# One flag in a planned kernel: the casts of dense operands offered to ScalarE during attention as well

## The chip, the cores and the metric

The kernel runs on one core of a Trainium2 chip. The metric is the device time of one execution in microseconds (us). The engines are TensorE (PE; its weight loads are PEld), VectorE (DVE), ScalarE (ACT), GpSimd (POOL) and SyncE (SP), which issues all transfers between the chip's memory and the core.

## The reference

Two computations stand side by side in the output, 2048 rows by 2 x 1024 columns, all in 32-bit floats.

```python
# left half: attention, 32 heads of 32 columns, no mask
qkv = (x @ wqkv)                       # x 2048x1024, wqkv 1024x3072
scores = einsum("bhqd,bhkd->bhqk", q, k) * Dh ** -0.5
o = einsum("bhqk,bhkd->bhqd", softmax(scores), v)
a = o_as_2048x1024 @ wo
# right half: a Fourier mixing with the matrices given as inputs
p = x2 @ hid_re.T ; q = x2 @ hid_im.T
b = seq_re @ p - seq_im @ q            # 2048x2048 by 2048x1024, twice
out = concatenate([a, b], axis=-1)
```

## The kernel before

**The dense products** (the projections to q, k and v; the two stages of the Fourier mixing, called dense1 and dense2; the output projection, called project) are done in blocks by a scheme with seven products in place of eight, so many operands are first sums or differences of blocks. They run on TensorE in a fast 32-bit format (`F32R`). To keep the accuracy each operand is split in two: the high part is the operand rounded to that format, the low part is what is left. Three matmuls are then made, high by high, low by high, high by low. An operand tile is 128 x 512. Its way is: a load by SP into `raw` (line 437); where it is a sum, a second load `g` (line 446) and an addition on GpSimd or VectorE (line 453); then in `halves` the **cast to the high part** on VectorE (line 475) or on ScalarE (line 473), and the subtraction for the low part on GpSimd or VectorE (line 478). Stationary operands are called `h` and `l` and live in three buffers (`piece`), moving operands are called `slot` (`moving`). The results of the q and k projection pass through `halves` too; their high part is `vh` early in the kernel and `e` later. Line 389 is the matmul of every dense product, into the PSUM tiles `pd` and `psT`; lines 627 to 745 and 892 to 910 take the results out.

**Attention** goes head by head. Line 1193 makes a 128 x 1024 piece of scores in PSUM (`psS`, two buffers). VectorE takes the row maximum, negated, `negm` (line 1199). ScalarE makes exp and its row sums from it, in place (line 1202), which frees the buffer. From these come the softmax's maxima and sums. Line 1316 makes the scores once more, transposed, 128 x 512 (`psT`, two buffers), with the maxima folded in as extra rows. ScalarE makes exp of them into one of 27 tiles `pt` and `ptl` (line 1320). Line 1335 multiplies these by V into `pd`, three times for each head after 5, 5 and 6 of its 16 rows of tiles; lines 1346 and 1348 gather the sums in `ot`, line 1364 divides by the softmax's sums, line 1366 stores them to `o_d`. The projection's operands are loaded from `o_d`, and no load of them starts before the stores of all heads are issued and done.

**The order** is made by a planner when the program is built, and nothing is decided on the chip. Each operation is an `Op` with an engine, a cost in us, a rank and the operations that it waits for. `Plan` keeps a list for each engine of what is ready; an engine that is free takes the ready operation of lowest rank. The row maximum has rank 0 on VectorE and the exps have -1 and 0 on ScalarE. An operation may have a second engine (`other`), and then stands in both lists, with its own cost and rank in each: the engine that is free first takes it, and where both are free ScalarE is asked before VectorE. The additions and subtractions have GpSimd and VectorE in this way. A cast has VectorE (cost 0.415, rank 10 + number of its group) and, where `spare[0]` is true at the time when the operation is set up, ScalarE too (cost `ACAST` = 0.6, rank 25 + number of its group). Operations with `two=True`, casts among them, are kept by the planner from running on VectorE while GpSimd runs. TensorE's own order is made by the loop from line 1396: the attention's three streams S (psS), T (psT) and V (times V), and the list `fills` of all dense matmuls in order. A fill goes where no stream is ready, or where the dense part is behind the pace (`nf / (FILL - RES) <= done / ATT`). The projection is the end of that list.

`qkv` sets up its dense products in twelve steps. The first five make the blocks that the first heads need; the rest of `qkv`, then dense1 and dense2, are worked off while attention runs, from about 245 to 2790 us. Line 804 sets the flag at the head of each of the steps 0 to 9: true in steps 0 to 4, and false from step 5, after which it stays false until `behind` (line 1064) sets it true for the projection.

Of the kernel before, what the change touches and what calls it, by code (L numbers as in the profile page):

```python
# [210 lines left out]
def kernel(  # L211
# [253 lines left out]
    spare = [True]  # L465
# [18 lines left out]
    def piece(terms, store=None):  # L484

        box = {}
        raw, made, users = fetch([P, 4, P], terms, store)
        (o0, u0), (o1, u1) = HR.take(), LR.take()

        def tile_of(key):  # L490
            def get():
                if key not in box:
                    box[key] = parts.tile([P, 4, P], F32R, name=key, tag=key, bufs=3)
                return box[key]
            return get

        h, l = tile_of("h"), tile_of("l")
        made = halves(raw, made, users, h, l, (o0, o1), (u0, u1), (HR, LR))
        both = Both(u0, u1)
        return Piece(h, l, made, both)  # L500
# [66 lines left out]
    def qkv():  # L567
# [5 lines left out]
        def w_terms(p, q, s_d, s):  # L573
            return {
                1: lambda: [(1, q(0, 0), [])], 2: lambda: [(1, q(0, 1), [])], 4: lambda: [(1, q(1, 1), [])],
                5: lambda: [(1, q(1, 0), []), (1, q(1, 1), [])],
                6: lambda: [(1, q(1, 0), []), (1, q(1, 1), []), (-1, q(0, 0), [])],
                7: lambda: [(1, q(0, 0), []), (-1, q(1, 0), [])],
                3: lambda: [(1, q(0, 1), []), (-1, s_d, s)],
            }[p]()  # L580
# [18 lines left out]
        def load_x(x, k):  # L599
            where[0] = ahead if x < 5 else within  # L600
            p = STEPS[x][0]
            if x < 5:
                i = 8 * ((x + 1) % 2) + k
                i = i if i < 12 else 20 + i
            else:
                i = (8 * (x - 5) + k) % 12 if x < 11 else (16, 8)[k // 4] + k
            XS[x, k] = moving(i, x_terms(p, k, x >= 5), (tx_d[k], tx[k]) if x == 3 else (t1x_d[k], t1x[k]) if x == 2 else None)

        def load_v_weight(x, c):
            where[0] = ahead if x < 5 else within  # L610
            p = STEPS[x][0]
            WV[x, c] = moving((28 if x in (1, 3) else 12 if x == 10 else 0 if x == 11 else 36) + c, w_terms(p, lambda i, j: wv[i, 4 * j + c], sv_d[c], sv[c]), (sv_d[c], sv[c]) if p == 6 else None)

        def acc(i):
            box = {}

            def get():
                if "t" not in box:
                    box["t"] = vp.tile([P, 2, NB], F32, name=f"acc{i}")
                return box["t"]  # L620

            return [Acc(get, [], [], k) for k in range(2)]
# [161 lines left out]
        def qk_group(x, W, b, n):  # L784
            p = STEPS[x][0]
            early = x < 5
            h = FIRST.get(p)
            if p == 1 and n == 0:
                if early:
                    X[2 * b], X[2 * b + 1] = acc(b)  # L790
                else:
                    X[2 * b], X[2 * b + 1] = accs(15 + b - PAIRS)
            group(((chunk(W, c), (XS[x, 4 * n + c], whole)) for c in range(4)), 4,
                  gather(p, 2 * b + n, qk_result(b + 8 * h[0], 2 * h[1] + n, early) if h else None, early, None if b % 2 else SCALE))

        def v_group(x, t):
            p = STEPS[x][0]
            h = FIRST.get(p)
            s0 = t % 4 * P
            group((((XS[x, 4 * (t // 4) + c], lambda u, s0=s0: u[:, s0 : s0 + P]), (WV[x, c], whole)) for c in range(4)), 4,  # L800
                  gather(p, 16 + t, v_result(h[0], 8 * h[1] + t, x < 5) if h else None, x < 5))

        for x, (p, blocks, v) in enumerate(STEPS[:10]):
            spare[0] = x < 5
            for i, b in enumerate(blocks):
                where[0] = ahead if x < 5 else within
                W = piece(w_terms(p, lambda i, j: wqk[b + 8 * i][:, 4 * j : 4 * j + 4, :], sq_d[b], sq[b]), (sq_d[b], sq[b]) if p == 6 else None)
                if x == i == 0:
                    first = W
                    for k in range(4):  # L810
                        load_x(0, k)
                    qk_group(x, W, 0, 0)
                    continue
                if x == 0 and i == 1 or x > 5 and i == 0:
                    for k in range(4, 8):
                        load_x(x, k)
                qk_group(x, W, b, 0)
                if x == 0 and i == 1:
                    qk_group(x, first, 0, 1)
                qk_group(x, W, b, 1)  # L820
                if x == 0:
                    if i == 1:
                        for c in range(4):
                            load_v_weight(0, c)
                elif x < 5:
                    for k in range(8 * i // len(blocks), 8 * (i + 1) // len(blocks)):
                        load_x(x + 1, k)
                elif i < 4:
                    load_x(x + 1, i)
            for t in range(8 if v else 0):  # L830
                if p == 1 and t % 2 == 0:
                    X[16 + t], X[17 + t] = acc(PAIRS + t // 2)
                v_group(x, t)
                if x == 0:
                    load_x(1, t)
                if t < 4 and x < 4:
                    load_v_weight(x + 1, t)
            where[0] = within
            if x == 4:
                for u in ahead[0].users + slots[28:]:  # L840
                    att_gate.extend(u)
                for i in range(12, 20):
                    slots[i] = list(att_gate)
            if x == 9:
                for c in range(4):
                    load_v_weight(10, c)
# [514 lines left out]
    def result(h, e, po, ouse):  # L1361
# [4 lines left out]
        o_st[h].append(op("SP", ISSUE, lambda: nc.sync.dma_start(o_d[h // 4][:, h % 4, :], po["o"]), [a], [ouse], -2, 256))  # L1366

    qkv()
    for w in (1, 0):
        for j in range(4):  # L1370
# [135 lines left out]
```

## Time and profile before

| | |
|---|---|
| three timed runs, median | 2978.28 us (2978.08 to 2978.9) |
| profiled execution, first to last instruction (span) | 2976.1 us |
| TensorE busy | 2950.9 us, 99% |
| VectorE busy | 2403.6 us, 81% |
| ScalarE busy | 2285.9 us, 77% |
| GpSimd busy | 868.7 us, 29% |
| casts on VectorE (line 475), whole span | 615 |
| casts on ScalarE (line 473), whole span | 161, none between 180 and 2800 us |

For the profiled execution the profile gives its span and no other time; the runs' median is 2.2 us above it.

How to read the lines that follow. A row of the groups names line, engine and operation, then the tile written and the tiles read, their shapes and the count; then busy time in us and the mean of one in ns; then the idle time of the engine just ahead of these instructions and what ended it. A row of busy times by stretch has the stretch, its length, then for PE, PEld, DVE, ACT and POOL the busy time with the number of instructions, then the granted TensorE clock, the share of the DMA engines and GB/s; where it is asked of one line only, the busy time is that of this line. A row of the waits names who waited, for whom, the us in total, how often, and the longest. A row of the view of one line has least, median and longest duration in ns, and the start of the first and last. A row in order of time has start, duration, engine, line, operation, and in brackets the idle time before it with what ended it. A row of the chain of waits has start, length, engine, tile, line and count.

### The profile page before, as it was taken

The page shows a single profiled execution, that of the slowest core. Times are in us where ns is not written, and L with a number is a line of the kernel's source. Part 1 is how long each engine was busy: PE and PEld are TensorE (multiplying, and loading weights), DVE is VectorE, ACT ScalarE, POOL GpSimd, SP SyncE. Part 2 cuts the span into 40 slices and gives each one's busy share as a digit, 9 for nine tenths or more (in the row PEclk, how much of TensorE's full clock was granted, in tenths as well). Part 3 has the DMA queues.
Part 4 walks back from the last instruction along what each step waited for, and adds up shares of the span by engine and source line. Part 5 has one row for each costly group of instructions (what it writes and reads, how often), then busy time and mean ns, then how long its engine had stood idle before and what let it go on. Part 6 is the DMA issues. An engine that isn't in the chain of part 4 may idle for free. (4 is left out here: it accounts for less than half of the span.)

```text
span 2976.1 us, 45423 instructions
## 1 busy us (share of the span) xinstructions
PE 2950.9 (99%) x14912; PEld 2136.2 (72%) x14912; DVE 2403.6 (81%) x3237; ACT 2285.9 (77%) x4314; POOL 868.7 (29%) x641
## 2 busy tenths in 40 slices
PE   9999999999999999999999999999999999999999
PEld 7886766777777777777777667677777666677787
DVE  7678889788877877777778898888777888887696
ACT  5347888888888888888888888888888888887431
POOL 2312425122212332131102443332012534342152
PEclk9999999999999999999999999999999999999999
DMA  9974658666625655554425775555334775555662
GB/s 347 357 228 161 196 181 284 220 218 227 209 74 193 193 155 160 172 177 149 153 87 170 226 226 166 162 165 164 113 110 137 228 248 174 160 181 179 229 229 98
DMA packets 376576, 558.56 MB, mean 188 GB/s; under 512 B 111100, under 2 KB 111100, under 8 KB 376220
## 3 DMA queue, kind: packets, MB, share of 16 engines
q1 hardware_dynamic: 376344, 555.68, 58.6%
q8 instruction: 120, 1.97, 0.3%
q14 instruction: 112, 0.92, 0.1%
HBM read 402.42 MB, written 153.11 MB: 187 GB/s over the span
## 5 line engine op out<-in xcount | busy, mean ns | idle before, releaser
L1199 DVE TENSOR_REDUCE negm<-psS 128x1 f32<-128x1024 f32 x1024 | 1240.6, 1219 | 194.8 <-PE psS L1193 189.6
L1202 ACT ACTIVATE psS<-psS,negm 128x1024 f32<-128x1024 f32 x1024 | 1170.7, 1143 | 104.2 <-DVE negm L1199 99.2
L1320 ACT ACTIVATE pt<-psT 128x512 f32<-128x512 f32 x1668 | 964.9, 654 | 270.7 <-PE psT L1316 268.6
L389 PE MATMUL pd<-slot,h 128*128 128x512 f32 x3368 | 1145.7, 390 | 1.2 <-DVE ot L1346 0.9
L1316 PE MATMUL psT<-qs,ks 128*128 128x512 f32 x2048 | 804.9, 396 | 0.0
L389 PEld LDWEIGHTS pd<-slot,h 128*128 128x128 f32 x3368 | 632.3, 188 | 133.7 <-DVE h L475 1.3
L389 PE MATMUL pd<-slot,l 128*128 128x512 f32 x1684 | 656.4, 390 | 0.7 <-POOL l L478 0.7
L1316 PEld LDWEIGHTS psT<-qs,ks 128*128 128x128 f32 x2048 | 381.6, 188 | 169.5 <-issue 62.9
L1193 PE MATMUL psS<-ks,qs 128*128 128x512 f32 x1552 | 476.2, 392 | 7.1 <-ACT psS L1202 6.5
L478 POOL TENSOR_TENSOR l<-raw,h 128x512 fp32r<-128x512 f32 x160 | 214.6, 1341 | 828.9 <-PE psT L1316 344.8
L1335 PE MATMUL pd<-pt,vt 128*32 128x512 f32 x3336 | 430.6, 594 | 0.2
L453 POOL TENSOR_TENSOR raw<-raw,g 128x512 f32<-128x512 f32 x216 | 285.7, 1329 | 439.1 <-issue 74.8
L389 PEld LDWEIGHTS pd<-slot,l 128*128 128x128 f32 x1684 | 316.2, 188 | 67.4 <-POOL l L478 1.0
L1193 PEld LDWEIGHTS psS<-ks,qs 128*128 128x128 f32 x1552 | 288.5, 188 | 76.4 <-ACT psS L1202 17.9
L478 POOL TENSOR_TENSOR slot<-raw,slot 128x512 fp32r<-128x512 f32 x143 | 206.6, 1453 | 432.9 <-DVE slot L475 203.1
L1335 PEld LDWEIGHTS pd<-pt,vt 128*32 128x32 f32 x3336 | 111.3, 110 | 230.2 <-issue 216.4
L1320 ACT ACTIVATE ptl<-psT 128x512 f32<-128x512 f32 x380 | 224.5, 654 | 59.9 <-PE psT L1316 59.5
L1202 ACT ACTIVATION_READ_ACCUMULATOR psS<-psS,negm 128x1 f32 x1024 | 266.6, 260 | 0.0
L389 PE MATMUL pd<-slot,slot 128*128 128x512 f32 x768 | 193.4, 390 | 0.0
L389 PEld LDWEIGHTS pd<-slot,slot 128*128 128x128 f32 x768 | 144.2, 188 | 30.8
L475 DVE CAST h<-raw 128x512 fp32r<-128x512 f32 x321 | 148.8, 464 | 14.8 <-PE pd L389 10.7
L1348 DVE TENSOR_TENSOR ot<-ot,pd 128x512 f32<-128x512 f32 x64 | 44.0, 687 | 144.0 <-PE pd L1335 143.9
(121 smaller groups left out, 2254.6 us busy)
## 6 DMA issues: line engine op xcount, KB each, us to landing
raw<-in_ct SPq DMA_DIRECT2D x224, 256.0 KB
g<-in_ct SPq DMA_DIRECT2D x128, 256.0 KB
qk_d<-e SPq DMA_DIRECT2D x52, 512.0 KB
qs<-qk_d SPq DMA_DIRECT2D x128, 192.0 KB
ks<-qk_d SPq DMA_DIRECT2D x128, 192.0 KB
raw<-ab_d SPq DMA_DIRECT2D x96, 256.0 KB
c<-u_d SPq DMA_DIRECT2D x88, 256.0 KB
g<-ab_d SPq DMA_DIRECT2D x80, 256.0 KB
```

What stands on the lines that cost most here:

```text
L389: nc.tensor.matmul(box["ps"], a[1]((a[0].hi, a[0].lo)[u]()), b[1]((b[0].hi, b[0].lo)[v]()), start=k == 0, stop=k == n - 1)
L453: (nc.gpsimd if e == "POOL" else nc.vector).tensor_tensor(out=dest(), in0=dest() if a is None else a.get(), in1=other["q"] if "q" in other ...
L475: nc.vector.tensor_copy(hi(), raw())
L478: (nc.gpsimd if e == "POOL" else nc.vector).tensor_tensor(out=lo(), in0=raw(), in1=f(hi()), op=ALU.subtract)
L1193: nc.tensor.matmul(p[:, i * NB : i * NB + NB], (QX[0] if own else QS[h % 2])[:, qt * P : qt * P + P], KS[h % 2][:, c * 1024 + i * NB : c * ...
L1199: nc.vector.tensor_reduce(out=ST["negm"][:, c, qt : qt + 1], in_=box["p"], axis=AX.X, op=ALU.max, negate=True)
L1202: nc.scalar.activation(box["p"], box["p"], AF.Exp, bias=ST["negm"][:, c, qt : qt + 1], accum_out=ST["sums"][:, c, qt : qt + 1])
L1316: nc.tensor.matmul(box["p"], KS[h % 2][:, t * P : t * P + P], QS[h % 2][:, j * NB : j * NB + NB], start=True, stop=True)
L1320: nc.scalar.activation(box["t"], box["p"], AF.Exp)
L1335: nc.tensor.matmul(po["p"][j * DH : j * DH + DH, :], VT[h][:, k, :], box["t"], start=(k == t0), stop=(k == t), tile_position=(0, j * DH),)
L1348: nc.vector.tensor_tensor(out=po["o"], in0=po["o"], in1=po["p"], op=ALU.add)
```

## The change

In `qkv`, line 804:

```diff
         for x, (p, blocks, v) in enumerate(STEPS[:10]):
-            spare[0] = x < 5
+            spare[0] = True
             for i, b in enumerate(blocks):
                 where[0] = ahead if x < 5 else within
```

The flag is then true from the start to the end. Every cast that is set up in the steps from 5 on, in dense1 and in dense2 is offered to ScalarE as well, with the cost and the rank that the first steps and the projection have. What is cast, added, subtracted, multiplied and stored is the same as before, on the same tiles; the planner makes a new order from it for all engines.

## The prediction

> **What bounds the kernel now.** I read the head of the page first, then busy times by stretch, then who waits for whom.
>
> ```profile
> span 2976.1 us, 45423 instructions
> ...
> PE 2950.9 (99%) x14912; PEld 2136.2 (72%) x14912; DVE 2403.6 (81%) x3237; ACT 2285.9 (77%) x4314; POOL 868.7 (29%) x641
> ```
>
> ```profile
> 74.00:148.00 74.00, 74.00 (x328) 61.29 (x327) 52.26 (x75) 26.05 (x44) 24.08 (x17) 1.00 0.98 359
> 245.00:2790.00 2545.00, 2530.19 (x13063) 1789.31 (x13065) 2066.16 (x2783) 2132.80 (x4059) 739.27 (x550) 1.00 0.57 178
> 2714.00:2791.00 77.00, 77.00 (x428) 51.93 (x426) 41.94 (x79) 40.44 (x76) 4.00 (x3) 1.00 0.53 165
> ```
>
> TensorE is idle for 2976.1 - 2950.9 = 25.2 us of the whole span, and its clock is full (the 1.00 in each stretch). A busy TensorE could still be one that creeps, so I check its pace: from 74 to 148 us 328 matmuls of 512 columns take 74 us, 0.226 us each, and the chain of waits on its last 130 us advances by 5.44 us for each 24 of them, 0.227 us:
>
> ```profile
> 2963.90 5.44 PE pd L389 x24
> ```
>
> So TensorE is the bound, and the change takes no matmul away. From 245 to 2790 us (attention) VectorE is idle for 2545 - 2066 = 479 us and ScalarE for 2545 - 2133 = 412 us. An engine relieved there gives time back only where TensorE waited for it:
>
> ```profile
> PEld psS L1193 <- ACT psS L1202: 30.7, 50, 1.7
> PEld psT L1316 <- ACT pt L1320: 9.7, 51, 0.3
> PEld psT L389 <- ACT slot L473: 6.3, 1, 6.3
> ```
>
> In the first row a score matmul into psS waits 50 times for an exp that has not yet read the bank; the second is the same for psT, 51 short waits. The third is the kernel's first matmul, before the change begins. 30.7 + 9.7 = 40.4 us, 1.4% of the span, is thus the ceiling of a gain, and all of it hangs on ScalarE. ScalarE in turn waits:
>
> ```profile
> ACT pt L1320 <- PE psT L1316: 268.6, 181, 6.7
> ...
> DVE ot L1348 <- PE pd L1335: 143.9, 58, 6.0
> ACT psS L1202 <- DVE negm L1199: 99.2, 136, 6.9
> DVE ot L1346 <- PE pd L1335: 67.0, 27, 4.3
> ```
>
> Two kinds of gap: 268.6 us in which it has no transposed score, and 99.2 us in which the row maximum (negm) from VectorE is late. The VectorE rows for ot show that a good part of the first kind is the P.V matmuls: 85 times (58 + 27) VectorE too stands still until they end, 211 us in all. While TensorE runs P.V it makes no scores, and both engines run dry together.
>
> **The change, part by part.** No instruction is added. A cast on offer to both engines goes to the one that the planner finds free first; it then writes down another order for all engines, the queues of DMAs included.
>
> ```profile
> 245.00:2790.00 2545.00, 276.52 (x576) 1.00 0.57 178
> ```
>
> That is line 475 in attention: 576 casts on VectorE, 0.480 us each. *How many move* the trace of before cannot show; the bounds are none and 576. ScalarE is idle for 412/2545 = 16% of the stretch, exps go before casts in its list, and VectorE, which also has the casts in its list, is idle beside it while P.V runs. I take 16% of 576 = 93, say 100.
>
> ```profile
> L475 DVE CAST h<-raw 128x512 fp32r<-128x512 f32 x321 | 148.8, 464 | 14.8 <-PE pd L389 10.7 <-issue 1.8 <-PE psT L389 1.0
> ...
> L453 DVE TENSOR_TENSOR raw<-raw,g 128x512 f32<-128x512 f32 x156 | 122.5, 791 | 18.8 <-DMA raw<-t_d 3.5 <-DMA raw<-in_xb 3.0 <-DMA g<-in_ct 2.9
> ...
> L475 DVE CAST slot<-raw 128x512 fp32r<-128x512 f32 x230 | 121.2, 541 | 1.5 <-DMA raw<-ab_d 0.6 <-PE pd L389 0.2
> ...
> L473 ACT ACTIVATE slot<-raw 128x512 fp32r<-128x512 f32 x54 | 32.2, 628 | 84.2 <-PE psT L389 33.2 <-DMA raw<-in_wo 17.0 <-issue 15.1
> ...
> L475 DVE CAST e<-e 128x512 fp32r<-128x512 f32 x52 | 26.5, 510 | 0.2
> ...
> L473 ACT ACT_TABLE_LOAD x1 | 1.3, 1283 | 0.7 <-PEq L1499 0.7
> ```
>
> *VectorE loses* 100 x 0.48 = 48 us of 2066. VectorE isn't the bound, so by itself this is worth 0.
>
> *ScalarE gains* 100 x 0.63 = 63 us beside 412 us of idle time. The cover is the gaps above and, for an exp that is pushed back, TensorE's dense matmuls, which the planner deals out meanwhile. There is no reload of function tables to pay: the whole span has one load, though copies (line 473) and exps alternate before 180 us. The planner charges 0.60 us for such a cast and the row says 0.63: 100 x 0.03 = 3 us of lateness that the written order does not know of. I charge all 3 us to TensorE.
>
> *A stall goes.* Casts on VectorE run 379/420/1514 ns (least, median, most) in one group:
>
> ```profile
> L475 DVE CAST h<-raw x307: 379/420/1514, 253.1 to 2784.1; 128x512 fp32r<-128x512 f32 x154
> L475 DVE CAST slot<-raw x217: 378/420/1552, 246.6 to 2756.8; 128x512 fp32r<-128x512 f32 x109
> ```
>
> ```profile
> 248.43 1.29 POOL L478 TENSOR_TENSOR e<-e 128x512 fp32r<-128x512 f32 x1
> ...
> 248.52 1.48 DVE L475 CAST slot<-raw 128x512 fp32r<-128x512 f32 x1
> ...
> 249.92 1.21 DVE L1199 TENSOR_REDUCE negm<-psS 128x1 f32<-128x1024 f32 x1
> ...
> 250.31 0.74 PE L1193 MATMUL psS<-ks,qx 128*128 128x512 f32 x2 [0.59 <-ACT psS L1202]
> ```
>
> The cast of 248.52 stands 1.06 us too long while a GpSimd subtraction runs, the next maximum starts late, and soon a score matmul waits. What casts lose in this way, against the 420 ns of the median: 321 x 0.044 + 230 x 0.121 + 52 x 0.090 = 14.1 + 27.8 + 4.7 = 47 us. With 100 of 576 moved, 8 us of it go. The additions of line 453 are stretched too, 791 ns against 0.69 us of one with no other by its side:
>
> ```profile
> 1298.18 0.69 DVE L453 TENSOR_TENSOR raw<-raw,g 128x512 f32<-128x512 f32 x1 [3.03 <-DMA raw<-in_xb]
> ```
>
> That is 156 x 0.10 = 16 us, and such delays and late loads together make the 30.7 us; at 30.7/(47 + 16) = 0.5 us of stall for each us of stretch, which is generous, 8 us give **-4 us**. Ends: 0, and -23 us if all casts moved (47 x 0.5). Late next is then the same maximum behind a stretched addition or subtraction, which stay where they are.
>
> The Trainium skill (page "SBUF — State Buffer", section "SBUF: two separate sides") says that VectorE and GpSimd share one pair of ports as an exclusive lock, the loser blocked for the whole instruction, while ScalarE has ports of its own. The pair at 248 us agrees, the cast ending just after the subtraction. By that rule each moved cast is one collision less; it is rival A below.
>
> *A wait is added.* ScalarE works in order: a cast whose raw tile is not there holds every exp behind it, those hold the psS and psT banks, and those hold TensorE. On VectorE the casts hardly wait for data (0.6 us for DMA raw<-ab_d in the row of slot<-raw): taken over, 0 us. Upper end: the additions on VectorE, which wait 18.8/156 = 0.12 us each, so 100 x 0.12 = 12 us. I take **+1 us**, near the cast rows since it is the same operation on the same tiles.
>
> *The rest is dealt again.* The order on all engines changes, SP's loads and stores with it, and the stalls that have nothing to do with casts fall elsewhere. The nearest rows give no sign to it: 0, with ends of half the 30.7 us to either side, 15 us.
>
> *The end.* The last head's P.V ends, then dense matmuls cover the way to the projection's operands:
>
> ```profile
> 2787.10 4.03 PE L1335 MATMUL pd<-pt,vt 128*32 128x512 f32 x34
> ...
> 2813.03 0.63 ACT L473 ACTIVATE slot<-raw 128x512 fp32r<-128x512 f32 x1 [1.34 <-DMA raw<-o_d]
> ...
> 2819.57 2.65 PE L389 MATMUL psT<-slot,slot 128*128 128x512 f32 x11
> ```
>
> From 2791.1 to 2819.6 lie 28.5 us of dense work; the operands' casts end at 2813.7, 6 us early. Before it, from 2714 to 2791, the last head has 77 us with ScalarE busy for 40.4, so 37 us of room. Attention may thus run some 37 + 6 = 43 us late before TensorE stands still at the end. 63 us of casts, most of them in gaps, stay below that: 0.
>
> **Sum** against the profiled execution: 2976.1 + 3 - 4 + 1 + 0 + 0 = 2976.1 us. The runs' median, 2978.28, is 2.2 us above this span, and that stays: 2978.3, rounded to **2978.5 us**. About 0.2%, 6 us, is what a measurement of this kernel can tell from no change.
>
> **Rivals.**
>
> A, *the collisions were the stall* (faster). ScalarE takes 250 casts or more: 250/576 x 47 = 20 us of stretch go, the cleared VectorE also makes the maxima earlier, and 8 to 20 of the 30.7 us vanish: 2958 to 2970, taken at 2966. For it: the pair at 248 us, and the maximum as what ScalarE waits for 136 times. Against it: VectorE is idle in the P.V gaps too and will often be first.
>
> B, *ScalarE's queue is held* (slower). Casts wait on loads and GpSimd sums as the additions do: 12 us, plus as much again from exps that find a cast begun just before them (100 x 0.12): 2978.3 + 12 to + 24, taken at 2992. It decides as soon as a cast's input lands later than ScalarE reaches it, in over a third of the moved casts. For it: TensorE's only sizeable waits are for ScalarE. Against it: ScalarE's own gaps of 1.5 us (268.6/181).
>
> C, *attention ends late* (slower). With 250 casts, half of them before an exp that was due, 125 x 0.63 = 79 us of delay meet 43 us of room: +36 us, 3014. It needs more than 43/0.63 = 68 casts that nothing hides.
>
> D, *the planner gives ScalarE next to nothing*, since VectorE is always first: 2978.3.
>
> **How the numbers follow.** Forecast (within 6 us) 0.44, D 0.05, A 0.21, B 0.20, C 0.10. So faster 0.21, same 0.49, slower 0.30. The forecast's own range is 2972 to 2985. For 8 in 10, A is taken in down to 2962 and B in full and C up to 3004; what is left out is the foot of A (0.05) and most of C (0.08).
>
> **What would show it.** Line 473 with some 100 more casts and line 475 with as many fewer; the exps' waits for psT and negm shorter by some 60 us together; the wait of psS matmuls for exps within 15 us of 30.7; TensorE's count of matmuls unchanged. A shows in that wait below 20 us and hardly any cast above 1 us; B in ScalarE waiting at line 473 for DMA or GpSimd inside attention, and that wait above 42 us; C in a gap of TensorE between the last P.V and the projection's first matmul. I am wrong if line 473 takes more than half of the casts, or if the order moves the loads so that TensorE waits for an operand (line 389).

## The result, and the profile after

The changed kernel takes **2984.63 us** (median of 17 runs, 2982.59 to 2987.87), the kernel before 2977.59 us in the same runs: a ratio of 1.0027, 95% interval 1.002 to 1.0034, some 7 to 8 us slower. The profiled execution went from 2976.1 to 2981.9 us, 5.8 more. First the page of the changed kernel and the view of line 473 inside attention:

```profile
span 2981.9 us, 45564 instructions
...
PE 2951.7 (99%) x14912; PEld 2141.9 (72%) x14912; DVE 2338.3 (78%) x3086; ACT 2349.1 (79%) x4444; POOL 894.9 (30%) x662
```

```profile
L473 ACT ACTIVATE h<-raw x54: 616/636/863, 246.1 to 2787.7; 128x512 fp32r<-128x512 f32 x54
L473 ACT ACTIVATE slot<-raw x47: 616/634/875, 246.6 to 2742.7; 128x512 fp32r<-128x512 f32 x47
...
L473 ACT ACTIVATE e<-e x7: 619/631/644, 249.5 to 737.8; 128x512 fp32r<-128x512 f32 x7
...
  PE pd L389: 9.5, 8
  DVE raw L453: 8.9, 11
```

54 + 47 + 7 = 108 casts went to ScalarE in attention. ScalarE stood still ahead of them, mainly for a free buffer (9.5 us) and for an addition on VectorE (8.9 us). TensorE makes the same matmuls at the same pace, so the question is where it waited. Its busy time in three stretches, before and then after:

```profile
200.00:800.00 600.00, 595.03 (x2995) 423.14 (x2994) 511.35 (x691) 495.69 (x939) 185.71 (x136) 1.00 0.66 214
800.00:2800.00 2000.00, 1990.16 (x10315) 1410.87 (x10314) 1601.12 (x2158) 1665.26 (x3171) 564.63 (x422) 1.00 0.54 165
2800.00:2850.00 50.00, 50.00 (x223) 41.39 (x222) 48.11 (x62) 18.21 (x30) 23.71 (x15) 1.00 1.03 367
```

```profile
200.00:800.00 600.00, 588.97 (x2958) 416.85 (x2957) 489.95 (x640) 502.56 (x950) 190.84 (x141) 1.00 0.66 211
800.00:2800.00 2000.00, 1996.38 (x10360) 1424.83 (x10362) 1567.38 (x2074) 1715.27 (x3277) 587.49 (x439) 1.00 0.54 166
2800.00:2850.00 50.00, 45.25 (x199) 34.81 (x188) 38.54 (x49) 20.41 (x35) 17.28 (x11) 0.94 0.90 319
```

Idle time of TensorE: 5.0 to 11.0 us in the first heads, 9.8 to 3.6 us in the long middle, 0 to 4.8 us where the projection begins, there with a granted clock of 0.94 besides. On this order the change is thus not one effect but three, and two of them nearly cancel.

A busy TensorE hides part of a wait, as its matmuls overlap in the trace (each counts as busy for 0.39 us and starts 0.23 us behind the one before). So I also add up, from the starts of the matmuls in the trace, what each start is later than the pace allows (0.2265 us after the one before; 0.318 us into and 0.522 us out of a run of P.V; distances within 20 ns of that are left out). I call this **lateness**. By it the stretches change by +8.4, -10.9 and +8.4 us, with 0.3 us in the first 200 us together +6.2. Span less lateness is 2933 to 2936 us in all fourteen kernels, so lateness is nearly the whole difference between them.

The middle shows as shorter waits of score matmuls (30.7 us before), the end as new rows:

```profile
PEld psS L1193 <- ACT psS L1202: 19.9, 34, 1.6
PEld psT L1316 <- ACT pt L1320: 12.8, 47, 1.4
PEld psT L389 <- ACT slot L473: 8.0, 2, 6.7
PEld psT L389 <- DVE slot L478: 5.1, 4, 4.0
```

This is the end in order of time, in the changed kernel:

```profile
2799.41 2.76 PE L1335 MATMUL pd<-pt,vt 128*32 128x512 f32 x24
...
2817.01 2.48 PE L389 MATMUL psT<-slot,slot 128*128 128x512 f32 x10
...
2840.42 0.73 PE L389 MATMUL psT<-slot,slot 128*128 128x512 f32 x2 [0.87 <-ACT slot L473]
...
2844.76 4.63 PE L389 MATMUL psT<-slot,slot 128*128 128x512 f32 x10 [3.60 <-DVE slot L478]
```

The last P.V ends at 2802.2 us, 11 us later than before, and the projection's first product begins only 15 us behind it (2817.01), where it was 28.5 us. Counted from the trace, 5983 dense matmuls now stand ahead of the last P.V's last matmul, 5923 before: 60 fewer are left to cover the loads. The first product gets by with a wait of 0.28 us; the second, due at 2839.4 us, finds its operands missing.

### The profile page after: what moved, and what is told of

The parts are those of the page before. It is cut to its first block, busy times and chain, and to the rows that moved or that the text cites. A ratio compares the mean times of both kernels' runs of the same rounds, so it can differ in the third digit from the quotient of the medians.

```text
span 2981.9 us, 45564 instructions
## 1 busy us (share of the span) xinstructions
PE 2951.7 (99%) x14912; PEld 2141.9 (72%) x14912; DVE 2338.3 (78%) x3086; ACT 2349.1 (79%) x4444; POOL 894.9 (30%) x662
## 4 chain that ended last, share of the span: by engine, by line
PE 93%; DVE 3%; DMA 2%; ACT 1%; issue 1%; POOL 0%; SPq 0%; DVEq 0%; POOLq 0%; ACTq 0%
PE pd L389 42%; PE psT L1316 15%; PE psS L1193 15%; PE pd L1335 15%; PE psT L389 6%; ACT psS L1202 1%; DVE negm L1199 1%; DMA raw<-in_ct 0%; DVE raw L453 0%; DMA raw<-tx_d 0%; DVE slot L475 0%; DMA raw<-in_wd 0%; ACT pt L1320 0%; DVE slot L478 0%; DMA qk_d<-e 0%
## 5 line engine op out<-in xcount | busy, mean ns | idle before, releaser
L1202 ACT ACTIVATE psS<-psS,negm 128x1024 f32<-128x1024 f32 x1024 | 1175.8, 1148 | 60.0 <-DVE negm L1199 56.8
L1320 ACT ACTIVATE pt<-psT 128x512 f32<-128x512 f32 x1668 | 966.8, 658 | 248.5 <-PE psT L1316 247.6
L478 POOL TENSOR_TENSOR l<-raw,h 128x512 fp32r<-128x512 f32 x170 | 226.7, 1333 | 870.8 <-PE psT L1316 300.2
L453 POOL TENSOR_TENSOR raw<-raw,g 128x512 f32<-128x512 f32 x208 | 278.2, 1343 | 375.8 <-DMA raw<-in_ct 73.1
L478 POOL TENSOR_TENSOR slot<-raw,slot 128x512 fp32r<-128x512 f32 x160 | 229.0, 1441 | 439.0 <-ACT slot L473 219.4
L1193 PE MATMUL psS<-ks,qx 128*128 128x512 f32 x496 | 150.4, 394 | 2.0 <-ACT psS L1202 1.9
```

What stands on the lines that cost most here:

```text
L453: (nc.gpsimd if e == "POOL" else nc.vector).tensor_tensor(out=dest(), in0=dest() if a is None else a.get(), in1=other["q"] if "q" in other ...
L478: (nc.gpsimd if e == "POOL" else nc.vector).tensor_tensor(out=lo(), in0=raw(), in1=f(hi()), op=ALU.subtract)
L1193: nc.tensor.matmul(p[:, i * NB : i * NB + NB], (QX[0] if own else QS[h % 2])[:, qt * P : qt * P + P], KS[h % 2][:, c * 1024 + i * NB : c * ...
L1202: nc.scalar.activation(box["p"], box["p"], AF.Exp, bias=ST["negm"][:, c, qt : qt + 1], accum_out=ST["sums"][:, c, qt : qt + 1])
L1320: nc.scalar.activation(box["t"], box["p"], AF.Exp)
```

## The experiments

My theory from the traces (three terms): the casts of the q, k and v steps cost 8 us in the first heads; the casts of dense1 and dense2 save 11 us in the middle; and attention that ends behind more dense work leaves the projection's loads uncovered, 8 us. Rival 1: ScalarE's queue is held by casts wherever they stand. Rival 2, called O below: the planner deals a new order and the three terms are its accidents. All kernels, lateness in us by stretch (up to 200 us and from 600 to 800 us are left out), and the count of dense matmuls ahead of the last P.V:

| kernel | median us | ratio to before, 95% | 200-500 | 500-600 | 800-2800 | from 2800 | first psT at | dense ahead |
|---|---|---|---|---|---|---|---|---|
| before | 2977.59 | | 10.1 | 1.7 | 27.7 | 0.0 | 247.6 | 5923 |
| after | 2984.63 | 1.0027 (1.002 to 1.0034) | 11.6 | 6.7 | 16.8 | 8.4 | 253.7 | 5983 |
| e1 q, k, v only | 2988.19 | 1.0031 (1.002 to 1.0043) | 12.0 | 7.2 | 23.5 | 4.4 | 254.4 | 5941 |
| e2 dense only | 2977.38 | 0.9994 (0.9985 to 1.0003) | 10.6 | 1.7 | 17.2 | 8.3 | 247.8 | 5983 |
| e3 before, faster pace | 2985.60 | 1.0026 (1.0016 to 1.0036) | 10.6 | 0.7 | 27.6 | 9.8 | 249.3 | 5994 |
| e4 after, swapped | 2977.89 | 0.9997 (0.9989 to 1.0006) | 13.3 | 5.4 | 18.2 | 0.7 | 253.0 | 5983 |
| e5 dense only, swapped | 2970.14 | 0.9974 (0.9965 to 0.9984) | 9.9 | 1.6 | 18.8 | 1.6 | 249.1 | 5983 |
| e6 before, swapped | 2977.26 | 1.0001 (0.9992 to 1.001) | 9.5 | 1.6 | 26.5 | 0.5 | 249.6 | 5923 |
| e7 as e4, not step 5 | 2986.59 | 1.0031 (1.002 to 1.0043) | 7.5 | 9.0 | 26.3 | 4.9 | 254.5 | 5998 |
| e8 as e4, line 1229 free | 2984.38 | 1.0025 (1.0014 to 1.0035) | 4.8 | 6.1 | 27.5 | 2.6 | 249.9 | 5995 |
| e9 as e6, line 1229 free | 2979.18 | 1.0007 (0.9997 to 1.0017) | 11.0 | 1.2 | 27.2 | 0.0 | 249.1 | 5896 |
| e10 as e5, line 1229 free | 2981.05 | 1.0013 (1.0004 to 1.0022) | 10.6 | 1.3 | 29.0 | 0.1 | 249.9 | 5947 |
| e11 as e6, evacuation 0.70 | 2982.78 | 1.0018 (1.0009 to 1.0027) | 9.7 | 3.8 | 27.7 | 0.0 | 249.0 | 5918 |
| e12 as e5, evacuation 0.70 | 2979.51 | 1.0007 (0.9998 to 1.0017) | 9.1 | 3.5 | 21.2 | 0.3 | 247.4 | 5973 |

**e1, the flag for the q, k and v steps only.** To the changed kernel:

```diff
     qkv()
+    spare[0] = False
     for w in (1, 0):
```

> The flag is true through the q, k and v projections and false for dense1 and dense2. Theory (three terms: TensorE waits about 8 us more while the first heads run, 11 us less from 800 to 2800 us, 8 us more in the projection): the first term stays, the other two go, so 2976 + 8 = 2984 to 2987 us, with line 473 between 800 and 2800 us empty. Rival 1 (ScalarE's queue is held by casts wherever they stand): the loss follows the number of casts in attention, some 30 of 108, so +2 us, 2979 to 2981. Rival 2 (the order is dealt anew and no term has a cause of its own): anything from 2970 to 2990.

2988.19 us, 1 us above the theory's range. The loss in the first heads is there in full (12.0 and 7.2), and rival 1's small loss is not what is seen. But the wait at the projection did not go altogether: 18 dense matmuls more than before stand ahead of the last P.V, and 4.4 us of lateness are left. That count alone does not explain it. The second product began 46 us behind the last P.V, which is later than it was due in the changed kernel (37 us), but TensorE's last wait for its operands ended only 52 us behind the last P.V. GpSimd stood still for 8.0 us there, for one load from `o_d`. How long the loads take is thus a matter of the order too. The middle moved as well, by 4 us, though no cast moved there.

**e2, the flag for dense1 and dense2 only.** To the kernel before:

```diff
     qkv()
+    spare[0] = True
     for w in (1, 0):
```

> The flag is false from step 5 of the q, k and v projections, as before, and true for dense1 and dense2. Theory: the first heads run as before (term 0), the middle gains 11 us, the projection still waits 8 us, so 2973 to 2977 us. Rival 1: some 80 of 108 casts stay in attention and three quarters of the loss with them, 2982 to 2984. Rival 2: 2970 to 2990.

2977.38 us, 0.4 us above the theory's range and outside rival 1's: the first heads are as before, the middle has its gain, the end its wait. Rival 1 falls.

**e3, the kernel before with a faster pace of the dense work.**

```diff
-    RES = 400
+    RES = 280
```

> The kernel before, with no cast more on ScalarE, but RES is 280 in place of 400, which holds dense matmuls to a faster pace, so that some 5990 of them in place of 5923 stand ahead of the last P.V. Theory (the projection waits because too little dense work is left to cover the loads of its operands, not because of casts): a wait of 8 to 12 us appears between 2810 and 2850 us, 2986 to 2990 us. Rival (the projection waits because its casts stand behind other casts on ScalarE): no wait there, 2976 to 2979 us.

2985.60 us, 0.4 us below the theory's range, and the wait is there without a cast moved. In order of time, in e3:

```profile
2846.43 0.73 PE L389 MATMUL psT<-slot,slot 128*128 128x512 f32 x2 [1.44 <-ACT slot L473]
2850.78 4.64 PE L389 MATMUL psT<-slot,slot 128*128 128x512 f32 x10 [3.61 <-DVE slot L478]
```

The same two waits as in the changed kernel, the longer one again 3.6 us, with 5994 dense matmuls ahead of the last P.V. The first product waits here too, 0.84 and 0.19 us. So the wait at the end needs no cast on ScalarE, only too little dense work behind attention.

**e4, the changed kernel with two products of the projection swapped.** The second product had twelve operand tiles that are differences (24 loads); now the one with twelve single loads comes second.

```diff
-            1: ([20, 24], 0), 7: ([4, 8], 20), 2: ([0, 4], 24), 6: ([8, 0], 20),
+            1: ([20, 24], 0), 2: ([4, 8], 20), 7: ([0, 4], 24), 6: ([8, 0], 20),
...
-        ORDER = (1, 7, 2, 6, 5, 3, 4)
+        ORDER = (1, 2, 7, 6, 5, 3, 4)
...
-                    if n != 7:
+                    if n != 2:
...
-                load_a(7, J0 + J1)
+                load_a(2, J0 + J1)
...
-                if x < 6 and i == 7 and ORDER[x + 1] != 7:
+                if x < 6 and i == 7 and ORDER[x + 1] != 2:
```

> The changed kernel, but in the projection the second product is the one whose twelve operand tiles are single loads, and the one whose twelve are differences of two loads comes third. Theory (the wait at the projection is the load of twice twelve tiles behind the last head's stores): the 8 us at 2840 us go, the rest stays, 2975 to 2978 us. Rival (the wait comes from casts on ScalarE or from VectorE): the number of casts is the same and the wait stays, 2983 to 2986 us.

2977.89 us, as the theory had it. The stretch of e4, where the changed kernel had 45.25 us busy and a clock of 0.94:

```profile
2800.00:2850.00 50.00, 49.73 (x238) 38.72 (x231) 38.77 (x47) 21.24 (x35) 17.58 (x12) 1.00 0.86 297
```

The rest of the order is the changed kernel's, and its other terms stay (first heads 13.3 and 5.4, middle 18.2). The wait at the end was the load of those tiles.

**e5, e2 with the swap, and e6, the kernel before with the swap.** The edits are those of e2 and e4.

> Flag true for dense1 and dense2 only, and the projection's single-load product second. Theory (the three terms are separate): early term 0, middle -11, projection 0 to 1, so 2966 to 2970 us, faster than both kernels by 8 to 11 us. Rival 2 (an order dealt anew, terms without causes of their own): the middle gain need not repeat, 2970 to 2985 us.

2970.14 us, 0.9974 (0.9965 to 0.9984): faster than both kernels, though at the edge of both theories (2966 to 2970, and 2970 to 2985 for O), so it does not choose between them.

> The kernel before, with the projection's products swapped and no cast moved. Theory: before has no wait at the projection, so nothing is to be had there, 2975 to 2979 us. Rival (the swapped order is simply shorter): 2968 to 2971 us.

2977.26 us: the swap alone gains nothing where nothing waited.

**e7 and e8, what happens in the first heads.** Once the last row maximum of head 0 is there, VectorE reduces, subtracts and transposes 128 x 16 and 128 x 32 tiles, two transfers follow, and then the first psT matmul may run. Before, and then after:

```profile
239.14 0.18 DVE L1226 TENSOR_REDUCE lh<-negm 128x16 fp32r<-128x32 f32 x1
240.47 0.16 DVE L1229 TENSOR_TENSOR lh<-nm,lh 128x16 fp32r<-128x16 f32 x1
...
247.64 0.63 PE L1316 MATMUL psT<-qs,ks 128*128 128x512 f32 x2
```

```profile
239.60 0.17 DVE L1226 TENSOR_REDUCE lh<-negm 128x16 fp32r<-128x32 f32 x1
242.07 1.29 POOL L478 TENSOR_TENSOR slot<-raw,slot 128x512 fp32r<-128x512 f32 x1 [1.00 <-ACT slot L473]
243.31 1.31 POOL L478 TENSOR_TENSOR l<-raw,h 128x512 fp32r<-128x512 f32 x1
244.25 0.40 DVE L1229 TENSOR_TENSOR lh<-nm,lh 128x16 fp32r<-128x16 f32 x1
...
253.67 0.40 PE L1316 MATMUL psT<-qs,ks 128*128 128x512 f32 x1
```

After the change ScalarE's casts feed GpSimd, GpSimd subtracts one tile behind another, and the small two-input subtraction of line 1229, which the planner keeps off VectorE while GpSimd runs, comes at 244.25 in place of 240.47. The first psT matmul follows 6 us later. e7 takes the casts of step 5 away from ScalarE, e8 lifts the rule for line 1229; both have the swap.

```diff
-            spare[0] = True
+            spare[0] = x != 5
```

> The changed kernel with the swapped products, and the flag false at step 5 alone, whose casts stand just ahead of the first transposed scores. Theory E (the early loss begins when ScalarE's casts feed GpSimd without a break, the small two-input subtraction of line 1229 is put back, and the first transposed score comes 6 us late): first transposed score at 247 to 249 us, waits from 200 to 300 us back at 5 us or less, 2 to 5 us less than with the swap alone in the early stretch. Rival F (the early loss is the loads of earlier results, c, that come late after 500 us in the new order): waits from 200 to 300 us may change, those from 500 to 600 us stay near 7 us.

2986.59 us. Theory E's first number fails: the first psT matmul is still at 254.5 us, so the casts of step 5 are not what holds it back. Yet its second number nearly holds: lateness from 200 to 300 us is 5.2 us, as in the kernel before (5.5), where the changed kernel has 7.3 and e4 8.9 (1.6 of these at a halved clock around 267 us). A first psT matmul that comes 7 us late thus need not cost TensorE anything. Rival F's mark holds: 9.0 us between 500 and 600.

```diff
-        c = op("DVE", TINY, low, [a, b], [nuse, luse], -2, two=True)
+        c = op("DVE", TINY, low, [a, b], [nuse, luse], -2)
```

> The changed kernel with the swapped products; the planner no longer keeps the 128 x 16 subtraction of line 1229 off VectorE while GpSimd runs, and nothing else is altered. Theory E: first transposed score at 246 to 250 us in place of 253, waits from 200 to 300 us at 5 us or less, total 2972 to 2976 us. Rival (the first score is late for ScalarE's exps and not for this subtraction): first transposed score stays at 253 us and the total at 2978 us.

The early wait went as theory E had it, and the total did not. In order of time, in e8:

```profile
241.79 0.17 DVE L1226 TENSOR_REDUCE lh<-negm 128x16 fp32r<-128x32 f32 x1
...
242.57 0.71 DVE L1229 TENSOR_TENSOR lh<-nm,lh 128x16 fp32r<-128x16 f32 x1
...
249.94 0.61 PE L1316 MATMUL psT<-qs,ks 128*128 128x512 f32 x2
```

The subtraction stands 0.8 us behind its reduction, and the first psT matmul is at 249.9; the lateness from 200 to 300 us falls from 8.9 us in e4 to 0.9. This is more than the change had cost there: the changed kernel has 7.3 us and the kernel before 5.5, so of the 8.4 us of the first heads line 1229 can account for 1.8. On the order without the flag the same edit takes nothing away (e9: 5.9 us). But 6.1 us between 500 and 600 stay, and the middle, which nobody touched, went from 18.2 to 27.5 us: 2984.38 us. What TensorE waits for around 515 us, in the changed kernel and then in e7 (505 to 530 us; before has no such row):

```profile
PE psS L1193 <- ACT psS L1202: 2.2, 3, 1.0
PE pd L389 <- DVE e L679: 1.1, 1, 1.1
```

```profile
PE pd L389 <- DVE e L679: 4.0, 2, 3.5
```

In the changed kernel the waits for exps (2.2 us) are longer than the one for line 679 (1.1 us). In the trace line 679 waits for its load of an earlier result (`c<-u_d`): 2.2 us in the changed kernel, 3.8 us in e7. In e8 TensorE waits 2.5 us for the same line, which there stands behind an addition that waited 2.4 us for another load (`raw<-tx_d`). Part of this lateness is no wait at all: after these waits the granted clock is halved for some 3.4 us in the changed kernel, e1 and e8 and for 6.8 us in e7 (see the last section), though not in e4. Lateness from 500 to 600 us is 5.4 to 9.0 us in all three orders that have the flag in the q, k and v steps (after with e1 and e4; e7; e8) and 0.7 to 1.7 us in most orders without it, but 3.5 and 3.8 in e11 and e12. With the flag, more dense matmuls have run by the time of a given head: 1603 in the changed kernel, 1629 in e7 and 1611 in e8 at the first psT matmul of head 4, against 1584. That dense work which runs ahead of the loads is the cause is only argued; no run took it away by itself.

Nor does the loss of the first heads repeat as a whole: from 200 to 800 us the lateness is 21.0, 17.4 and 12.6 us in three orders with the flag there (after, e7, e8) and 12.6, 14.3 and 16.7 us in three without (before, e9, e11). Whether the flag or the particular order makes the 8.4 us is open.

**e9 to e12, is the gain in the middle the casts' or the order's?** The changed kernel and e4 share one order in the second half of attention, and e2 and e5 another that differs from it little (the counts of dense matmuls at each head are the same from head 16 on). Their agreement on the middle is thus one observation, not four. So I made two pairs that differ in the flag for dense1 and dense2 alone, each on an order of its own: e9 and e10 with e8's edit, e11 and e12 with the planner's charge for taking results out of PSUM altered.

```diff
-    MAX, EVAC, CAST, BIT = 1.22, 0.685, 0.415, 0.275
+    MAX, EVAC, CAST, BIT = 1.22, 0.7, 0.415, 0.275
```

> First of two pairs that differ in the flag for dense1 and dense2 alone, each on an order of its own. No flag; swapped products; the subtraction of line 1229 may run beside GpSimd. Theory M (casts taken off VectorE shorten TensorE's waits from 800 to 2800 us): about 27 us of waits there, as in the kernel before. Theory O (the waits there are what an order happens to have, by 17 to 28 us, whoever makes the casts): anything from 17 to 30. Total 2972 to 2982.

> The same with the flag true for dense1 and dense2. Theory M: 8 to 11 us fewer waits from 800 to 2800 us than in e9, total 2966 to 2972, faster than e9. Theory O: no fewer than in e9 by more than 4 us, or more. Both: more dense matmuls ahead of the last P.V than in e9, by some 50.

> Second pair, no flag: swapped products, and the planner's charge for taking a result out of PSUM is 0.70 in place of 0.685 us, which alters nothing but the order. Theory M: about 27 us of waits from 800 to 2800 us. Theory O: anything from 17 to 30. Total 2972 to 2982.

> The same with the flag true for dense1 and dense2. Theory M: 8 to 11 us fewer waits from 800 to 2800 us than in e11, total 2966 to 2972. Theory O: no fewer than in e11 by more than 4 us, or more. Both: some 50 dense matmuls more ahead of the last P.V than in e11.

The flag changes the middle by +1.8 us (27.2 to 29.0) in the first pair and by -6.5 us (27.7 to 21.2) in the second; e5 against e6 is -7.7. e7 and e8, with 78 and 71 casts on ScalarE from 800 to 2800 us where the changed kernel has 82, have 26.3 and 27.5. The waits of score matmuls in e9 and then in e10:

```profile
PEld psS L1193 <- ACT psS L1202: 29.6, 50, 1.9
```

```profile
PEld psS L1193 <- ACT psS L1202: 34.0, 53, 1.9
```

Theory M, 8 to 11 us for the casts, is not what the pairs show. O's mark, at most 4 us fewer, holds in the first pair and fails in the second. An order's middle is late by 17 to 29 us with the flag and by 26 to 28 without; whether some small gain is left on average stays open. What an order alone can do is seen in e11: it moves no cast, and takes 5 us more than e6 (2982.78 to 2977.26). What repeats in every pair is the other thing: 60, 51 and 55 dense matmuls more ahead of the last P.V with the flag.

## Why the prediction was right or wrong

The forecast was no change, 2978.5 us, with 2972 to 2985 us as its own range. 2984.63 us lies inside it by 0.4 us, and that is luck. The interval of the ratio, 1.002 to 1.0034, tells the 7 us from none, and the three terms behind them, +8.4, -10.9 and +8.4, have neither the causes nor the sizes of the terms in the sum.

**What bounds the kernel**: right. TensorE's pace didn't change, but for some 10 us at a halved clock, and lateness is all that moved. But the ceiling held for a gain only, and the loss came at places where hardly anything had waited before.

**How many casts move**: 100 were predicted, 108 moved, and rival D falls with it. VectorE's busy time in attention fell by 2066.2 - 2016.0 = 50 us (48 predicted) and ScalarE's rose by 2180.1 - 2132.8 = 47 us (63; 4 us of its exps now lie behind 2790 us), from this row of the changed kernel:

```profile
245.00:2790.00 2545.00, 2530.35 (x13056) 1797.96 (x13055) 2016.03 (x2664) 2180.13 (x4161) 764.04 (x570) 1.00 0.57 178
```

**The cast's price**: 631 to 636 ns in the median, as taken from the rows, and up to 875 ns. That the planner's 0.60 costs TensorE 3 us is shown by no run.

**A stall goes, -4 us** (and rival A): not shown. The middle did lose 10.9 us, but other orders with the same casts moved lose nothing, so it cannot be booked as the price of a cast. The step from the stretch of casts to TensorE's waits is what was not shown. The stretch itself shrank about as forecast: by the prediction's own count from 47 to 40 us, where 8 us were to go. A cast that stayed on VectorE is no freer of GpSimd for it, 504 ns in the mean of the three groups against 497 before, and one group is slower:

```profile
L475 DVE CAST slot<-raw 128x512 fp32r<-128x512 f32 x171 | 95.8, 574 | 0.6 <-PE pd L389 0.2
```

574 ns in the mean against 541 before. GpSimd is as much beside VectorE as it was (739 to 764 us busy in attention); I take it that a subtraction which waited for its cast now follows sooner, which no run shows. A's sign came out half: the wait for psS is 19.9 us, just below its 20, but 28 of the 467 casts left to VectorE in attention are still above 1 us (35 of 576 before).

**A wait is added, +1 us** (and rival B): ScalarE does wait at line 473, 9.5 + 8.9 us and some single waits, 0.2 us a cast, more than the 0 to 0.12 I gave. In the view of that line TensorE's weight loads wait 3.3 us for its casts. B as a whole falls with e2, whose 90 casts on ScalarE cost nothing in sum.

**The rest is dealt again, 0 with 15 us to either side**: the size was right. It was the term that mattered, and I gave it no place. Two pieces of it can be placed, line 1229 (up to 1.8 us) and the waits around 515 us, line 679 among them, with the halved clock behind them (5.0 us more than before from 500 to 600); what makes them stays open.

**The end, 0**: this is the step that failed. I held that attention might run 43 us late before TensorE stands still: 37 us in which ScalarE is idle in the last head, and 6 us by which the first product's operands were early. It ran 11 us late, and TensorE lost 8.4 us. The 37 us were no room at all: in the last head of the kernel before (2714 to 2791 us) 30.4 of them are waits for transposed scores that TensorE has not made, and being idle there does not end attention sooner. And of the margin I looked at the wrong product. The second product's operands take twice the loads. In the kernel before the last of the tiles that this product begins with was done at 2840.3 us and the product began at 2841.3, so the margin was 1 us and not 6. In the changed kernel and in e3 TensorE's last wait for these operands ended 42 to 43 us behind the last P.V (2844.8 less 2802.2, 2850.8 less 2809.1), where the kernel before asked for them 50 us behind it. 60 dense matmuls at 0.2265 us, 13.6 us, use that up. Nor is lateness of attention the measure: in e2 the last P.V ends only 3 us later than before (2794.3) and TensorE loses the same 8.3 us, as the same 60 matmuls are gone.

**Rival C** had half of the mechanism, TensorE standing at the projection, with a wrong cause and a wrong size: I let it begin at 68 casts that nothing hides and cost 36 us. It comes with the 90 casts of e2 and with none in e3, what counts is the dense work already spent, and it costs 8 us.

**The signs**: the exps' waits for psT and negm are shorter by 63 us together (268.6 + 99.2 to 247.6 + 56.8; some 60 predicted), and the wait for psS and TensorE's count of matmuls are as foretold. But one sign of being wrong that I gave, TensorE waiting for an operand of line 389 because the order moved the loads, is just what happened at the projection.

## What to carry to other kernels

Where an order is planned as a whole, compare the two traces stretch by stretch before believing a small total, and repeat an effect on a second and third order before giving it a cause: orders that share their second half are one observation. Here only the end passed this test: the flag puts more dense work ahead of the last P.V in every pair, e3 makes the wait without a cast, and e4 removes it. Idle time of a helper engine in the last stage is no slack; slack is the distance from the last result to the first instruction that needs what hangs on it, taken for every load in that queue and not for the first. The fastest kernel here, e5 at 0.9974 (0.9965 to 0.9984), moves the casts only where no head start is at stake and puts the product with fewer loads behind attention; the same idea on two other orders came out at 1.0013 and 1.0007 (e10 and e12), so its 8 us belong to that order. What the idea brings is a short end, 0.1 to 1.6 us of lateness in these three. It has a limit as well: in e7 and e8, with 5998 and 5995 dense matmuls ahead of the last P.V, the projection's first product waited, and the end cost 4.9 and 2.6 us.

## What the runs showed of the hardware

One wait of 3.6 us costs TensorE more than itself. Busy time in steps of 2 us in the changed kernel, TensorE's first, the granted clock third from the right:

```profile
2842.00:2844.00 2.00, 0.00 (x0) 0.00 (x0) 2.00 (x2) 1.49 (x3) 1.55 (x1) 0.91 1.04 389
2844.00:2846.00 2.00, 1.24 (x3) 1.05 (x4) 2.00 (x5) 1.15 (x2) 0.64 (x1) 0.50 1.06 393
2846.00:2848.00 2.00, 2.00 (x6) 1.52 (x6) 2.00 (x2) 0.00 (x0) 1.05 (x1) 0.50 1.06 389
2848.00:2850.00 2.00, 2.00 (x6) 1.56 (x5) 0.77 (x2) 0.00 (x0) 0.00 (x0) 0.50 1.05 386
2850.00:2852.00 2.00, 2.00 (x9) 1.62 (x8) 1.32 (x3) 0.00 (x0) 0.00 (x0) 0.89 1.05 386
```

The row of 2842 to 2844 us (0.91) puts the fall at about 2843.6, 2.5 us into the wait, and that of 2850 to 2852 (0.89) the return at about 2850.5. In between the clock is 0.50 and the matmuls start 0.427 us apart in place of 0.227: thirteen of them, 2.6 us on top of the wait. The wait of 0.87 us just before (2840.42) had left it at 1.00.

It does not take so long a wait. The same kernel has the clock at half some 500 us into the span as well:

```profile
522.00:524.00 2.00, 1.63 (x4) 1.30 (x5) 1.91 (x4) 2.00 (x5) 0.00 (x0) 0.64 0.71 197
524.00:526.00 2.00, 2.00 (x6) 1.52 (x6) 0.81 (x1) 1.74 (x5) 1.27 (x1) 0.51 0.96 369
```

From 522.6 to 526.0 us the matmuls are 0.427 us apart, and no wait in the 20 us ahead of them is longer than 1.1 us; there are four of 0.6 to 1.1 us within 11 us (512.1, 513.9, 520.3 and 522.4).

The Trainium skill (page "TensorE: Matmul & The Clock Gate", section "Part 1: The HAM clock gate") says that the array falls to half clock after an idle window of about 3.4 us and returns after as long a busy one. The trace agrees as to the half clock. It differs in the rest: the clock fell 2.5 us into one wait and without any wait above 1.1 us in the other case, and it stayed at half for 6.8 us in the first and 3.4 us in the second.
